# Loading the first tokens in two halves, casting in quarters, and a new order of issue in a fused attention and maxout kernel

## The chip, the cores and the metric

One core of one Trainium2 chip. The metric is the device time of one execution in microseconds (us), median of several runs. "Span" is the length of the profiled part of an execution; the device time of a run is 1.7 to 3.3 us longer than its span. A run has a state: "slow" runs (here those over 1.5% above the fastest of the same kernel) are kept out of every ratio. A ratio is the mean time of one kernel's fast runs over the mean of the other's fast runs of the same rounds, so it is not quite the ratio of the medians quoted beside it; the brackets are its 95% interval.

In the profiles PE is TensorE (the array that multiplies) and PEld its weight loads, DVE is VectorE, ACT is ScalarE, POOL is GpSimd, and SP is SyncE, which here only issues transfers. A transfer has "landed" when all of it has arrived. "Before" and "after" name the kernel before the change and the changed kernel.

## The reference

Cut to what matters:

```python
# x: (8, 8, 512, 64)   state: (8, 8, 32, 64)     B, H, S, Ns, D = 8, 8, 512, 32, 64
def _attn_ref(x, state):
    scores = scale * np.matmul(x, state.transpose(0, 1, 3, 2))
    a = softmax(scores)                      # over the 32 states
    xread = np.matmul(a, state)              # 512 rows a batch
    scores2 = scale * np.matmul(state, x.transpose(0, 1, 3, 2))
    a2 = softmax(scores2)                    # over the 512 tokens
    sread = np.matmul(a2, x)                 # 32 rows a batch
    return np.concatenate([xread, sread], axis=2)

def _moe_ref(x, w1, w2, w3, w_out):          # 4352 rows of 512, d_ff = 768
    h = np.maximum(np.maximum(x @ w1, x @ w2), x @ w3)
    return h @ w_out
```

## The kernel before

The kernel never forms `xread`. It multiplies the state into the three weight matrices once per batch (`M`), and a token's 32 softmax weights per head then meet that product directly (`u`). The work is cut into small units, and a text lists them in order. The first batches have a hand-found list (OPENING); later batches repeat PERIOD, and the end has LAST. No scheduler reorders anything: each engine runs its instructions in this order, so an instruction that waits holds up all behind it on its engine.

```python
OPENING = """
id, idle 9, sel, idle 9, pm 0 0 a, pm 0 1 v, lx 1, xT 0 0 v, lw 2 4, pm 1 1 v, pm 1 0 v,
xT 0 1 a, idle 8, lw 1 2, lw 0 1, S 0 0 g, S 0 1 g, xT 1 1 a, xT 1 0 a, R 0, lw 4 6,
S 1 1 g, aT 0 0 a, M 0 2 va, aT 0 1 v, S 1 0 g, M 0 3 aa, M 1 3 av, M 1 2 aa, M 2 1 vv,
u 0 3 0, u 0 3 1, M 0 1 aa, u 0 2 0, M 1 1 va, aT 1 - v, u 0 2 1, M 0 0 aa, R 1, u 0 1 0,
... (cut: seven more lines)
"""
```

The words:

- `idle n`: n matmuls on zeros (`pz`) that keep the array warm. `sel`: the state, transposed on PE into `pst` and copied into the block-diagonal `sbd`, two copies on ACT and two on DVE.
- `pm b h e`: cast or permute tokens of batch b into `xn` on engine e. `xT b h e`: transpose that half of `xn` on PE (`px`) and copy it out on e. `xb b`: the same for a whole batch by a DMA that transposes ("the crossbar"), issued from SP.
- `S b h g`: scores on PE (`ps`), exponential on ACT (`e`), sum and reciprocal on DVE (`den`, `rden`), product on GpSimd (`a`). `aT b`: `a` transposed on PE (`pa`). `ab b`: the same by the crossbar.
- `M b m`: state times column block m of the weights (`pm` on PE, copies to `M_sb` on two engines). `u b m i`: two matmuls (`pw`) and one step of the maximum. `o b j h`: half an output tile (`po`). `R b`: the reads of the states (`pr`).
- `lx b`, `lw m0 m1`, `lo`: loads of tokens, of weight columns and of the output weights, all issued by GpSimd and cast to bf16 on the way.

The two loads that do not come from GpSimd stand ahead of the list:

```python
    st32 = res.tile([128, Ns // 2, D], F32, name="st32")
    nc.sync.dma_start(
        out=st32.rearrange("p n d -> p (n d)"),
        in_=state.rearrange("b h (q n) d -> (b h q) (n d)", q=2))
    x32 = res.tile([128, H, J, D], F32, name="x32")
    nc.sync.dma_start(out=x32.rearrange("p h j d -> p h (j d)"),
                      in_=x[0].rearrange("h (p j) d -> p h (j d)", j=J))
    ...
    nc.scalar.copy(out=st16, in_=st32)

    def load_w(m0, m1):
        c = slice(m0 * 128, m1 * 128)
        for i in range(3):
            nc.gpsimd.dma_start(out=W[:, i, :, c], in_=w_v[i][:, :, c])

    def load_x(b):
        x_sb[b] = xlp.tile([128, H, J, D], BF16, tag="x", name="x")
        nc.gpsimd.dma_start(
            out=x_sb[b].rearrange("p h j d -> p h (j d)"),
            in_=x[b].rearrange("h (p j) d -> p h (j d)", j=J))
    ...
    def x_crossbar(b):
        nc.sync.dma_start_transpose(
            out=xT(b).rearrange("p j hp t -> p (j hp) t"),
            in_=x_nat(b).rearrange("p j h d -> p (j h) d"))
```

The softmax here doesn't subtract the row's maximum and nothing guards it: scores larger than these inputs give would overflow.

Of the kernel before, what the change touches and what calls it, by code (L numbers as in the profile page):

```python
# [8 lines left out]
F32 = mybir.dt.float32  # L9
# [15 lines left out]



OPENING = """
id, idle 9, sel, idle 9, pm 0 0 a, pm 0 1 v, lx 1, xT 0 0 v, lw 2 4, pm 1 1 v, pm 1 0 v,
xT 0 1 a, idle 8, lw 1 2, lw 0 1, S 0 0 g, S 0 1 g, xT 1 1 a, xT 1 0 a, R 0, lw 4 6,  # L30
S 1 1 g, aT 0 0 a, M 0 2 va, aT 0 1 v, S 1 0 g, M 0 3 aa, M 1 3 av, M 1 2 aa, M 2 1 vv,
u 0 3 0, u 0 3 1, M 0 1 aa, u 0 2 0, M 1 1 va, aT 1 - v, u 0 2 1, M 0 0 aa, R 1, u 0 1 0,
lx 3, u 1 1 0, u 0 2 2, u 0 0 0, u 1 1 1, M 0 5 aa, M 0 4 aa, lx 2, u 0 1 1, u 0 3 2, lo,
u 1 3 0, u 0 0 1, u 0 5 0, M 1 0 va, pm 2 - g, u 1 3 1, u 1 1 2, u 0 4 0, M 2 2 aa,
u 1 3 2, lx 4, u 0 5 1, pm 3 - g, u 1 0 0, M 2 5 aa, M 1 5 aa, xb 3, u 0 1 2, u 0 5 2,
u 1 2 0, xT 2 1 v, u 0 4 1, u 0 0 2, u 1 5 0, u 0 4 2, xT 2 0 a, u 1 0 1, S 2 1 g,
o 0 0 0 v, M 1 4 aa, M 2 3 aa, o 0 0 1 v, u 1 2 1, o 0 1 0 v, S 2 0 g, u 1 5 1, u 1 2 2,
o 0 1 1 a, o 0 2 0 v, o 0 2 1 a, M 2 0 aa, M 2 4 aa, aT 2 - v, u 1 4 0, u 1 0 2, u 1 5 2,
o 0 3 0 v, o 0 3 1 a, u 1 4 1, u 1 4 2, R 2
"""  # L40


PERIOD = """
u u u P L S S o o u M M m o u u o u u u o u u o X u M m m R u o u u u o u u
"""
LAST = """
u u u u u u M M u u u S u o u o u u M u u R u u M o u o S M L o M P o o X o
"""


# [1 line left out]
def kernel(  # L52
# [14 lines left out]
    nc = tc.nc  # L67

    B, H, S, D = x.shape
# [5 lines left out]
    J = S // 128  # L75
# [8 lines left out]
    res = ctx.enter_context(tc.tile_pool(name="res", bufs=1))  # L84
# [14 lines left out]
    def copy(eng, o, i):  # L99
        if eng == "a":  # L100
            nc.scalar.copy(out=o, in_=i)  # L101
        else:
            ENG[eng].tensor_copy(out=o, in_=i)  # L103
# [4 lines left out]
    def tr(out_ap, in_ap):  # L108
# [4 lines left out]



    st32 = res.tile([128, Ns // 2, D], F32, name="st32")
    nc.sync.dma_start(
        out=st32.rearrange("p n d -> p (n d)"),
        in_=state.rearrange("b h (q n) d -> (b h q) (n d)", q=2))

    x32 = res.tile([128, H, J, D], F32, name="x32")
    nc.sync.dma_start(out=x32.rearrange("p h j d -> p h (j d)"),
                      in_=x[0].rearrange("h (p j) d -> p h (j d)", j=J))
    zeros = const.tile([128, 512], BF16, name="zeros")
    nc.vector.memset(zeros, 0.0)  # L125
    sbd = res.tile([128, B, HP, 2, Ns], BF16, name="sbd")
# [2 lines left out]
    nc.vector.memset(ones, 1.0)  # L129
    ident = const.tile([128, 128], BF16, name="ident")  # L130
    st16 = res.tile([128, Ns // 2, D], BF16, name="st16")
    nc.scalar.copy(out=st16, in_=st32)


    W = res.tile([128, 3, HP, d_ff], BF16, name="W")
# [5 lines left out]
# [5 lines that stand above are left out]
    def load_wout():  # L146
        nc.gpsimd.dma_start(out=wout, in_=moe_w_out.rearrange("(kk p) f -> p kk f", p=128))

    x_sb = {}
# [8 lines that stand above are left out]
    def idle(n):  # L158
        pz = bank([128, S], F32, "pz")
        for _ in range(n):  # L160
            mm(pz, zeros[:, 0:128], zeros, True, True)


    def state_to_T():
        sel = ident.rearrange("p (q a k) -> p a q k", a=2, k=2)
        for half in range(2):
            pst = bank([128, 8, 64], F32, "pst")
            for n in range(8):
                for par in range(2):
                    mm(pst[par * 64:(par + 1) * 64, n, :], st16[:, 8 * half + n, :], sel[:, par],  # L170
                       n == 0, n == 7, pos=(0, par * 64))
            for par in range(2):
                r = slice(par * 64, par * 64 + 64)
                o = sbd[r, :, :, par, :].rearrange("p b hp (k n) -> p (b hp) k n", k=2)
                copy("av"[par], o[:, :, :, 8 * half:8 * half + 8],
                     pst[r].rearrange("p n (q k) -> p q k n", k=2))
# [17 lines left out]
    def tile_of(kind, b, pool, shape):  # L194
        if (kind, b) not in tiles:
            tiles[kind, b] = pool.tile(shape, BF16, tag=kind, name=kind)
        return tiles[kind, b]

    def x_nat(b):
        return tile_of("xn", b, xnp, [128, J, H, D])  # L200
# [12 lines left out]

    def permute_x(b, h, eng):
        j = slice(0, J) if h is None else slice(2 * h, 2 * h + 2)
        i = x_sb[b][:, :, j] if b else x32[:, :, j]
        copy(eng, x_nat(b)[:, j], i.rearrange("p h j d -> p j h d"))

    def x_crossbar(b):
        nc.sync.dma_start_transpose(  # L220
            out=xT(b).rearrange("p j hp t -> p (j hp) t"),
            in_=x_nat(b).rearrange("p j h d -> p (j h d)"))

    def x_array(b, h, eng):
        px = bank([128, 2, HP, 128], BF16, "px")
        for jj in range(2):
            for hp in range(HP):
                tr(px[:, jj, hp, :], x_nat(b)[:, 2 * h + jj, 2 * hp:2 * hp + 2, :])
        copy(eng, xT(b)[:, 2 * h:2 * h + 2], px)
# [118 lines left out]
    def issue(words):  # L348
        op_, args = words[0], words[1:]
        n = [None if v == "-" else int(v) for v in args if v == "-" or v.isdigit()]  # L350
        eng = args[-1] if args and args[-1].isalpha() else None
        if op_ == "idle":
            idle(*n)
        elif op_ == "id":
            make_identity(nc, ident)
        elif op_ == "sel":
            state_to_T()
        elif op_ == "lx":
            load_x(*n)
        elif op_ == "lw":  # L360
            load_w(*n)
        elif op_ == "lo":
            load_wout()
        elif op_ == "pm":
            permute_x(*n, eng)
        elif op_ == "xb":
            x_crossbar(*n)
        elif op_ == "xT":
            x_array(*n, eng)
        elif op_ == "S":  # L370
            scores(*n, eng)
        elif op_ == "R":
            state_reads(*n)
        elif op_ == "ab":
            a_crossbar(*n)
        elif op_ == "aT":
            a_array(*n, eng)
        elif op_ == "M":
            made.add(tuple(n))
            m_unit(*n, eng)  # L380
        elif op_ == "u":
            up(*n)
        else:
            out_half(*n, eng)

    for unit in OPENING.split(","):
        issue(unit.split())

    m_q = [(b, m) for b in range(2, B) for m in range(MT) if (b, m) not in made]
    for t in range(1, B):  # L390
        p, g = ORDER[t], ORDER[t + 1]
# [60 lines left out]
```

## Time and profile before

| before | |
|---|---|
| device time, median of 3 runs | 160.18 us (160.11 to 160.54) |
| span of the profiled run | 158.2 us |
| PE busy | 150.8 us |
| state, then x of batch 0, landed | 4.07, 7.66 us |
| first scores, second `a` done | 11.41, 15.65 us |
| first `pw` (the first unit `u`) | 18.04 us |
| start of the repeated part (its first `pw`, by the chain of waits) | 47.23 us |
| one period | 15.77 us |
| last matmul ends | 154.79 us |
| last matmul to the end of the span | 3.4 us |

Read it by milestones. Once PE has work without holes, everything later follows from how much work is left, so each cause can be placed between two milestones. The prediction below shows the lines behind the table.

### The profile page before, as it was taken

The numbers are of one execution on the slowest core, as the hardware profiler recorded it, in microseconds if no ns is written. First come the engines' busy times: TensorE is split into PE (matmuls) and PEld (weight loads), VectorE is DVE, ScalarE is ACT, GpSimd is POOL, SyncE is SP. The second block draws the span as 40 slices with busy tenths as digits, with TensorE's granted clock in tenths as the row PEclk, the third lists the DMA queues.
The fourth block names the chain that finished last, engine by engine and source line by source line (L and its number), as shares of the span: only waits on it lengthen the run. The fifth ranks groups of instructions, "written<-read, shape, count | busy, mean of one in ns | idle before, by whom it ended". The sixth has DMA issues, their size and how long they took to land.

```text
span 158.2 us, 3558 instructions
## 1 busy us (share of the span) xinstructions
PE 150.8 (95%) x1387; PEld 76.1 (48%) x1404; DVE 112.0 (71%) x200; ACT 94.8 (60%) x188; POOL 44.3 (28%) x48
## 2 busy tenths in 40 slices
PE   6988899999999999999999999999999999999991
PEld 2456353354454454445444544444445567754450
DVE  3358999797669788968886888688868834378601
ACT  3549978768546765676477647764777433344340
POOL 8927960282630920190018001300130000000000
PEclk9999999999999999999999999999999999999999
DMA  5999999979659498909991609260316033030253
GB/s 161 279 195 188 185 162 163 200 104 173 195 60 250 116 198 114 264 29 181 126 265 38 167 0 244 68 161 0 137 46 153 4 133 133 0 133 4 66 188 143
DMA packets 34400, 21.46 MB, mean 136 GB/s; under 512 B 19536, under 2 KB 31824, under 8 KB 34384
## 3 DMA queue, kind: packets, MB, share of 16 engines
q0 software_dynamic: 14400, 6.82, 34.0%
q1 hardware_dynamic: 19840, 14.29, 32.9%
q8 instruction: 11, 0.18, 0.4%
q10 hardware_dynamic: 144, 0.13, 0.2%
q14 instruction: 5, 0.04, 0.1%
HBM read 15.20 MB, written 8.91 MB: 152 GB/s over the span
## 4 chain that ended last, share of the span: by engine, by line
PE 88%; DMA 4%; ACT 2%; POOL 1%; issue 1%; DVE 1%; SPq 0%; POOLq 0%
PE pw L106 45%; PE po L106 28%; PE pm L106 6%; DMA x<-in_x_dram 4%; PE pr L106 4%; PE ps L106 2%; PE px L109 1%; POOL a L246 1%; PE pz L106 1%; PE pa L109 1%; ACT e L238 1%; ACT xn L101 1%; ACT M_sb L101 0%; DVE den L242 0%; DVE oh L103 0%
## 5 line engine op out<-in xcount | busy, mean ns | idle before, releaser
L106 PE MATMUL pw<-aT,M_sb 128*128 128x512 bf16 x288 | 71.9, 379 | 0.0
L106 PE MATMUL po<-wout,ht 128*128 128x512 bf16 (+1 forms) x194 | 51.1, 373 | 0.8
L304 DVE TENSOR_TENSOR t<-t,pw 128x512 bf16<-128x512 bf16 (+1 forms) x54 | 35.4, 656 | 19.6 <-PE pw L106 9.1
L300 ACT CAST t<-pw 128x512 bf16<-128x512 f32 (+1 forms) x54 | 30.5, 567 | 29.5 <-PE pw L106 28.6
L106 PEld LDWEIGHTS <-M_sb 128*128 128x128 bf16 x288 | 26.9, 98 | 31.5 <-issue 1.0
L306 DVE TENSOR_TENSOR ht<-t,pw 128x512 bf16<-128x512 bf16 (+1 forms) x54 | 35.2, 657 | 6.8 <-PE pw L106 3.0
L246 POOL TENSOR_TENSOR a<-e,rden 128x512 bf16<-128x512 bf16 x16 | 16.4, 1041 | 59.4 <-ACT e L238 36.6
L101 ACT CAST M_sb<-pm 128x384 bf16<-128x384 f32 x75 | 30.9, 504 | 1.3 <-PE pm L106 0.5
L106 PEld LDWEIGHTS <-ht 128*128 128x128 bf16 x210 | 19.6, 98 | 21.3 <-issue 1.9
L101 ACT COPY o<-po 128x512 f32<-128x512 f32 x32 | 18.8, 586 | 18.6 <-PE po L106 16.1
L103 POOL COPY xn<-x 128x2048 bf16<-128x2048 bf16 x6 | 11.3, 1887 | 8.1 <-DMA x<-in_x_dram 8.1
L106 PE MATMUL pm<-W,sbd 64*32 64x384 bf16 x384 | 12.4, 327 | 0.5 <-ACT M_sb L101 0.4
L242 DVE TENSOR_REDUCE den<-e 128x16 f32<-128x512 bf16 x16 | 10.6, 661 | 2.0 <-ACT e L238 1.9
L238 ACT ACTIVATE e<-ps 128x512 bf16<-128x512 f32 x16 | 8.9, 598 | 4.6 <-PE ps L106 4.6
L103 DVE CAST M_sb<-pm 128x384 bf16<-128x384 f32 x21 | 10.6, 534 | 0.0
L144 POOL DMA_DIRECT2D W<-in_moe_w_dram x12 | 9.0, 771 | 3.6 <-DMA x<-in_x_dram 3.0
L106 PE MATMUL pw<-AT,W 128*128 128x256 bf16 x72 | 9.2, 273 | 0.1
L106 PE MATMUL pz<-zeros 128*128 128x512 bf16 x25 | 7.8, 470 | 1.2 <-DVE zeros L125 1.2
L106 PEld LDWEIGHTS <-sbd 64*32 64x32 bf16 x384 | 4.3, 89 | 9.7 <-issue 9.1
L106 PEld LDWEIGHTS <-W 128*128 128x128 bf16 x72 | 7.0, 98 | 2.5
L279 DVE RECIPROCAL rd<-pr 128x128 f32<-128x128 f32 x8 | 7.6, 947 | 0.2 <-PE pr L106 0.2
L153 POOL DMA_DIRECT2D x<-in_x_dram x7 | 6.6, 942 | 0.1
(39 smaller groups left out, 67.6 us busy)
## 6 DMA issues: line engine op xcount, KB each, us to landing
out_dram<-o SPq DMA_DIRECT2D x14, 512.0 KB, 2.9
x<-in_x_dram POOLq DMA_DIRECT2D x7, 512.0 KB, 7.7
W<-in_moe_w_dram POOLq DMA_DIRECT2D x6, 256.0 KB, 8.0
x<-in_x_dram SPq DMA_DIRECT2D x1, 1024.0 KB, 6.5
W<-in_moe_w_dram POOLq DMA_DIRECT2D x6, 128.0 KB, 10.9
wout<-in_moe_w_out_dram POOLq DMA_DIRECT2D x1, 768.0 KB, 12.6
out_dram<-o SPq DMA_DIRECT2D x3, 256.0 KB, 2.1
st<-in_state_dram SPq DMA_DIRECT2D x1, 512.0 KB, 3.3
```

Source lines behind the costliest of these rows:

```text
L101: nc.scalar.copy(out=o, in_=i)
L103: ENG[eng].tensor_copy(out=o, in_=i)
L106: nc.tensor.matmul(out_ap, lhsT, rhs, start=start, stop=stop, tile_position=pos)
L144: nc.gpsimd.dma_start(out=W[:, i, :, c], in_=w_v[i][:, :, c])
L153: nc.gpsimd.dma_start(out=x_sb[b].rearrange("p h j d -> p h (j d)"), in_=x[b].rearrange("h (p j) d -> p h (j d)", j=J))
L238: nc.scalar.activation(out=e.rearrange("p r n -> p (r n)"), in_=ps.rearrange("p j a hp n -> p (j a hp n)"), func=AF.Exp, scale=scale)
L242: nc.vector.reduce_sum(out=den, in_=e, axis=AX.X)
L246: ENG[eng].tensor_mul(out=a_of(b)[:, 2 * h:2 * h + 2].rearrange("p j a hp n -> p (j a hp) n"), in0=e, in1=rden.unsqueeze(2).to_broadcast(( ...
L279: nc.vector.reciprocal(out=rd, in_=pd.rearrange("p (hp n) -> p hp n", hp=HP))
L300: nc.scalar.copy(out=t[:, :nn], in_=pw[:, :nn])
L304: nc.vector.tensor_max(t[:, :nn], t0[:, :nn], pw[:, :nn])
L306: nc.vector.tensor_max(ht[:, m, :nn], tiles["t", g, m][:, :nn], pw[:, :nn])
```

## The change

Its intent: get batch 0 through its softmax sooner, by letting casts and transposes of a first half of x begin while the rest still loads; take transposes of batch 2 off PE; and find the orders anew for that.

```diff
+    x32 = res.tile([128, H, J, D], F32, name="x32")
     st32 = res.tile([128, Ns // 2, D], F32, name="st32")
+    def load_x32(k):
+        nc.sync.dma_start(
+            out=x32[:, :, 2 * k:2 * k + 2, :].rearrange("p h j d -> p h (j d)"),
+            in_=x[0].rearrange("h (p k j) d -> k p h (j d)", k=2, j=2)[k])
+    load_x32(0)
     nc.sync.dma_start(
         out=st32.rearrange("p n d -> p (n d)"),
         in_=state.rearrange("b h (q n) d -> (b h q) (n d)", q=2))
-    nc.sync.dma_start(out=x32..., in_=x[0]...)          # (cut)
+    load_x32(1)
-    nc.scalar.copy(out=st16, in_=st32)
+    def permute_x32(h, q, eng):                          # "p0 h q e": a quarter of x
+        j, hh = slice(2 * h, 2 * h + 2), slice(4 * q, 4 * q + 4)
+        copy(eng, x_nat(0)[:, j, hh], x32[:, hh, j].rearrange("p h j d -> p j h d"))
+    def cast_state(h, eng):                              # "ca h e": half of the state
+        n = slice(8 * h, 8 * h + 8)
+        copy(eng, st16[:, n], st32[:, n])
 OPENING = """
-id, idle 9, sel, idle 9, pm 0 0 a, pm 0 1 v, lx 1, xT 0 0 v, lw 2 4, pm 1 1 v, pm 1 0 v,
-...
+id, idle 9, p0 0 0 v, p0 0 1 a, xT 0 0 v, lw 2 4, ca 0 a, idle 5, p0 1 0 a, ca 1 v, lx 1,
+p0 1 1 v, sel, lw 1 2, lw 4 6, xT 0 1 v, S 0 0 g, S 0 1 g, pm 1 1 g, lw 0 1, M 0 3 vv,
+M 1 2 aa, M 1 3 aa, pm 1 0 v, R 0, aT 0 0 a, M 0 2 aa, lx 2, xT 1 0 a, aT 0 1 v,
+xT 1 1 v, M 0 1 va, lx 3, u 0 2 0, u 0 2 1, S 1 1 g, S 1 0 g, u 0 3 0, u 0 1 0, u 0 1 1,
+M 0 5 av, lo, M 0 4 aa, M 1 1 aa, u 0 3 1, u 0 2 2, u 0 3 2, pm 2 - g, u 0 4 0, M 0 0 aa,
+... u 1 4 0, xb 2, u 0 5 1, M 2 1 aa,
+... o 0 0 0 a, u 1 2 1, S 2 0 g, S 2 1 g, o 0 0 1 a, o 0 1 0 v, o 0 1 1 a, u 1 0 1, ab 2,
+...                                                      (cut)
 PERIOD = """
-u u u P L S S o o u M M m o u u o u u u o u u o X u M m m R u o u u u o u u
+P u u u S o u u S L o o o u u u m M m o o u u m m M R X u u u u u o o u u u
```

LAST is reordered too.

More of the change, by code (lines that the diff above doesn't have):

```diff
@@ L28 @@
 OPENING = """
-id, idle 9, sel, idle 9, pm 0 0 a, pm 0 1 v, lx 1, xT 0 0 v, lw 2 4, pm 1 1 v, pm 1 0 v,
-xT 0 1 a, idle 8, lw 1 2, lw 0 1, S 0 0 g, S 0 1 g, xT 1 1 a, xT 1 0 a, R 0, lw 4 6,
-S 1 1 g, aT 0 0 a, M 0 2 va, aT 0 1 v, S 1 0 g, M 0 3 aa, M 1 3 av, M 1 2 aa, M 2 1 vv,
-u 0 3 0, u 0 3 1, M 0 1 aa, u 0 2 0, M 1 1 va, aT 1 - v, u 0 2 1, M 0 0 aa, R 1, u 0 1 0,
-lx 3, u 1 1 0, u 0 2 2, u 0 0 0, u 1 1 1, M 0 5 aa, M 0 4 aa, lx 2, u 0 1 1, u 0 3 2, lo,
-u 1 3 0, u 0 0 1, u 0 5 0, M 1 0 va, pm 2 - g, u 1 3 1, u 1 1 2, u 0 4 0, M 2 2 aa,
-u 1 3 2, lx 4, u 0 5 1, pm 3 - g, u 1 0 0, M 2 5 aa, M 1 5 aa, xb 3, u 0 1 2, u 0 5 2,
-u 1 2 0, xT 2 1 v, u 0 4 1, u 0 0 2, u 1 5 0, u 0 4 2, xT 2 0 a, u 1 0 1, S 2 1 g,
-o 0 0 0 v, M 1 4 aa, M 2 3 aa, o 0 0 1 v, u 1 2 1, o 0 1 0 v, S 2 0 g, u 1 5 1, u 1 2 2,
-o 0 1 1 a, o 0 2 0 v, o 0 2 1 a, M 2 0 aa, M 2 4 aa, aT 2 - v, u 1 4 0, u 1 0 2, u 1 5 2,
-o 0 3 0 v, o 0 3 1 a, u 1 4 1, u 1 4 2, R 2
+id, idle 9, p0 0 0 v, p0 0 1 a, xT 0 0 v, lw 2 4, ca 0 a, idle 5, p0 1 0 a, ca 1 v, lx 1,
[3 more added lines that the diff above has]
+M 0 5 av, lo, M 0 4 aa, M 1 1 aa, u 0 3 1, u 0 2 2, u 0 3 2, pm 2 - g, u 0 4 0, M 0 0 aa,
+u 0 1 2, aT 1 - v, u 0 4 1, M 1 4 aa, M 1 0 av, u 0 4 2, u 0 0 0, u 1 1 0, u 0 5 0,
+u 1 1 1, u 0 0 1, u 1 3 0, u 1 0 0, u 0 0 2, u 1 3 1, u 1 4 0, xb 2, u 0 5 1, M 2 1 aa,
+M 2 4 aa, pm 3 - g, M 1 5 vv, u 0 5 2, u 1 1 2, u 1 2 0, u 1 3 2, xb 3, u 1 5 0,
+o 0 0 0 a, u 1 2 1, S 2 0 g, S 2 1 g, o 0 0 1 a, o 0 1 0 v, o 0 1 1 a, u 1 0 1, ab 2,
+M 2 2 aa, M 2 5 aa, u 1 0 2, R 1, o 0 2 0 v, o 0 2 1 a, u 1 4 1, lx 4, u 1 5 1, M 2 0 va,
+M 2 3 aa, R 2, u 1 4 2, u 1 2 2, o 0 3 0 v, u 1 5 2, o 0 3 1 a
 """
 PERIOD = """
-u u u P L S S o o u M M m o u u o u u u o u u o X u M m m R u o u u u o u u
+P u u u S o u u S L o o o u u u m M m o o u u m m M R X u u u u u o o u u u
 """
 LAST = """
-u u u u u u M M u u u S u o u o u u M u u R u u M o u o S M L o M P o o X o
+u u M u M M u X M M u P u u u u o u u u L u o u u u S S R u o u o M o o o o
 """
@@ L119 @@
         in_=state.rearrange("b h (q n) d -> (b h q) (n d)", q=2))
-    x32 = res.tile([128, H, J, D], F32, name="x32")
-    nc.sync.dma_start(out=x32.rearrange("p h j d -> p h (j d)"),
-                      in_=x[0].rearrange("h (p j) d -> p h (j d)", j=J))
+    load_x32(1)
     zeros = const.tile([128, 512], BF16, name="zeros")
@@ L215, in permute_x @@
         j = slice(0, J) if h is None else slice(2 * h, 2 * h + 2)
-        i = x_sb[b][:, :, j] if b else x32[:, :, j]
-        copy(eng, x_nat(b)[:, j], i.rearrange("p h j d -> p j h d"))
+        copy(eng, x_nat(b)[:, j], x_sb[b][:, :, j].rearrange("p h j d -> p j h d"))
+    def permute_x32(h, q, eng):
[4 more added lines that the diff above has]
+        copy(eng, st16[:, n], st32[:, n])
     def x_crossbar(b):
@@ L363, in issue @@
             load_wout()
+        elif op_ == "ca":
+            cast_state(*n, eng)
+        elif op_ == "p0":
+            permute_x32(*n, eng)
         elif op_ == "pm":
```

## The prediction

> **What bounds the kernel now.** I read the page first, then the chain of waits, the DMA of single microseconds, and the timeline of the opening. The page's busy row and its slices:
>
> ```profile
> PE 150.8 (95%) x1387; PEld 76.1 (48%) x1404; DVE 112.0 (71%) x200; ACT 94.8 (60%) x188; POOL 44.3 (28%) x48
> ...
> PE   6988899999999999999999999999999999999991
> ...
> DMA  5999999979659498909991609260316033030253
> ```
>
> PE has work in every slice from the sixth to the last but one; the first five, some 20 us, are not full although part of their work is filler (`pz` on zeros). The chain of waits says where PE takes over:
>
> ```profile
> 1.20 6.46 DMA x<-in_x_dram
> 7.68 1.05 ACT xn L101
> 8.78 1.07 PE px L109 x16
> ...
> 14.61 1.05 POOL a L246
> 15.71 0.40 PE pa L109 x4
> 16.10 0.25 PE ps L106 x8
> 16.37 0.60 ACT e L238
> 16.97 0.76 ACT M_sb L101 x2
> 17.75 0.36 PE pm L106 x8
> 18.11 0.97 PE pw L106 x4
> ```
>
> Until 18.11 the chain hops between DMA, casts, softmax and transposes; from there to 154.8 it is PE, back to back. So the time is (end of the last hole in PE) + (work then left on PE) + (a tail of 3.4 us of copy and store). The change can only gain by closing holes before 18 us or by taking work off PE.
>
> A second limit hides there. The landings of the weights (start of issue plus time to landing, asked one issue at a time):
>
> ```profile
> x<-in_x_dram POOLq DMA_DIRECT2D x1, 512.0 KB, 9.0
> ...
> W<-in_moe_w_dram POOLq DMA_DIRECT2D x1, 256.0 KB, 10.5
> ...
> W<-in_moe_w_dram POOLq DMA_DIRECT2D x1, 128.0 KB, 11.4
> ...
> W<-in_moe_w_dram POOLq DMA_DIRECT2D x1, 256.0 KB, 6.7
> ```
>
> x of batch 1: 1.43 + 9.0 = 10.4. Third piece of W for column blocks 2 and 3 (call it W23): 3.98 + 10.5 = 14.5. Third piece of block 1 (W1): 6.21 + 11.4 = 17.7. W0, by the same sum, 19.9. W45: 17.1 + 6.7 = 23.8. M_sb of block 1 first runs at 17.75, just when W1 lands. The queue that GpSimd feeds is full from 7 to 22 us:
>
> ```profile
> q1 hardware_dynamic: 92, 0.09, 103.9%
> q0 software_dynamic: 3, 0.00, 4.5%
> ...
> q0 software_dynamic: 788, 0.39, 145.4%
> ```
>
> The first two rows are 6.25 to 6.5 us, the third 10 to 12. The GpSimd queue moves nothing until the SP queue's 1.5 MB of state and x runs out, then 0.195 MB/us as counted on the bf16 side.
>
> **What the Trainium skill says.** "DMA: Bandwidth & Descriptors", section "Issuing engines are not separate DMA queues": all issuers share the 16 engines and interleave. The trace agrees on the sharing, but shows the SP queue served nearly alone first. The same page, "Why small descriptors are slow (HBM only)", gives a fixed 3 cycles per packet; halving x's runs from 1024 to 512 bytes would then cost (16+3)/16 against (32+3)/32, 9%. Here W1's small pieces ran at 714 packets per us in 16 to 17 us, 512 bytes read each, 365 GB/s, so I expect little loss. "VectorE: DVE Perf Modes", "The three transpose paths": a DMA transpose avoids PE but is slower in itself (1309 against 390 ns per 128x128). Here the crossbar of xT takes 4.4 to 6.7 us to land, all beside PE. "TensorE: Matmul & The Clock Gate", "What's actually happening": the array starts at half clock until busy some 3.4 us. Here the first 9 fillers took 4.02 us, the next 8 1.90; 9 fillers are kept at the start, so the array should be warm as before.
>
> **The change part by part.**
>
> 1. Head. The order of SP's queue becomes half of x, state, half of x. State and x landed at 4.05 and 7.66; the three equal pieces should land near 4.2, 6.0 and 7.8. Casts in quarters: 1024 columns took 1.04 us on ACT, 0.69 on DVE; half as many I estimate at 0.62 and 0.43 (slopes from 512- and 1024-column copies of aT). First half of x: cast by 4.9, transposed once the 9 fillers end at 5.2, copied by 6.5 on DVE. State: cast 6.0 to 7.0, 5 fillers, transposes 6.9 to 7.9. Second half of x: cast 7.8 to 8.5. But the two sbd copies on each engine stand behind these casts: DVE 8.3 to 9.6. Scores then start at 9.65 (before: 11.41), the second half after its xT copy at 10.35. The whole softmax chain moves up by about 1.8 us: second `a` done at 13.8 instead of 15.65.
>
> 2. GpSimd's queue. W23 goes ahead of x1, and W45 ahead of W0; bytes up to W1 are the same. At the old pace: W23 11.8 (was 14.5), x1 14.5 (was 10.4), W1 17.7 (as before), W45 17.7 + 0.786/0.195 = 21.7 (was 23.8), W0 about 24 (was 19.9).
>
> 3. PE in its new order, which cannot overtake. M 0 3, M 1 2, M 1 3 (8 matmuls, 0.25 to 0.29 us each) start at 11.8; R 0 takes 0.92, the first aT and M 0 2 end at 14.3. The array then waits for x1, cast and transposed by 16.2, then in M 0 1 for W1: 17.75. The first `pw` is at about 18.05, as now. Five `u` (0.43 each) and two scores (0.47) fill to 20.7; M 0 5 waits for W45 until 21.7, a hole of 1.0 us that the old order lacks.
>
> 4. Work taken from PE: 16 transposes of x and 8 of `a` for batch 2 go to the crossbar. They stand in the chain as 0.58, 0.45 and 0.55 us: 1.58 us gone. 12 of 26 fillers go too, but lay in holes.
>
> Sum: from M 0 5 at 21.7 to the end of the opening remain 31 `u` at 0.4315 (13.4), 13 M (3.2), 8 half outputs at 0.65 (5.2), two R (1.75), two scores (0.47), one aT (0.55): 24.6, so 46.3, plus 0.4 for changes of shape as the old opening shows (22.6 measured against 22.05 added up): 46.7. The old opening ends at 47.23. Gain 0.5 us.
>
> 5. The repeated period. It holds 18 `u`, 8 half outputs, 6 M, R and two scores in both orders: 7.77 + 5.18 + 1.22 + 0.92 + 0.47 = 15.56 by the chain's pieces, against 15.77 from 67.21 to 82.98. At most 0.2 us a period is there to win. DVE gets one more M copy (0.53) per period, 12.7 to 13.2 of 15.77; walking the new order I find its backlog behind R at 2 us, three or four of eight banks, hence no stall. Tail: the last `u`, halves and stores are the same. I put 0 on both.
>
> **The rivals.** (a) The earlier softmax is worth its full 1.8 us, plus the 1.58: 156.8. For it: the chain shows softmax ahead of 18.11. Against: W1 lands at 17.7 whatever the softmax does. It needs the loads to be quicker than I think. (b) Weights bind harder: W0 is now last, or small runs slow the head; M 0 0 waits beyond 24, and each microsecond of lateness is one of time: 161 to 162. (c) The crossbar for batch 2 is late: x2 lands near 26.5, GpSimd copies it (1.89), and with 6.3 to 6.7 to landing it ends near 35; scores of batch 2 stand at 35.5. Only about 0.5 us of slack; wout (34.3 before) meets `po` at 34.4 just as tightly. A slip would cost up to 1 us. (d) The new period runs worse, DVE at 84%: 0.2 us each in five periods, plus 1.0.
>
> **Range and chances.** My sum gives 160.2 - 0.5 = 159.7; (b) to (d) push up by perhaps 0.3, while an order found anew presumably survived some measure of its finder, and (a) in part would give 1 us or more. I choose 159.4. The landings of W1 and W45 carry plus or minus 0.8 each, which gives 157.8 to 160.8 for 8 in 10. Faster by over 2% needs below 157.0, all of (a) with no new hole: 0.08. Slower by over 2%, above 163.4, needs (b) and (c) together: 0.02. Within 2%: 0.90.
>
> **What would show it.** Right: first scores near 9.7; W23 landed near 11.8, W45 near 21.7; the first `pw` within 0.5 us of 18.1; holes in PE before M 0 1 and M 0 5 ending with W; the period at 15.7 to 15.8; 24 fewer transposes on PE. Wrong: `pw` starting below 17 with no hole at M 0 5 (rival a), a hole at `ps` of batch 2 or at the first `po` (c), or a period that differs by over 0.1 (d, or an unlooked-for gain). My prediction falls if the weights land over 1 us from my sums, since all of it hangs on their cumulative bytes.

## The result

| | before | after |
|---|---|---|
| device time, median of 6 runs each, same rounds | 160.5 us (160.11 to 160.8) | 162.18 us (161.97 to 163.44) |
| ratio | | 1.0117 [1.0084, 1.0151] |
| second half of x landed (before: all of x) | 7.66 | 9.83 |
| first scores, second `a` done | 11.41, 15.65 | 12.34, 16.77 |
| first `pw` | 18.04 | 19.05 |
| start of the repeated part | 47.23 | 48.31 |
| one period | 15.77 | 15.77 |
| last matmul ends | 154.79 | 155.92 |
| last matmul to the end of the span | 3.4 | 4.2 |
| device time less span, mean | 1.77 | 2.52 |

The changed kernel is slower, within 2%. The loss is 1.9 us (0.0117 of 160.4). In means over runs it has two parts: the span grows by 1.16 us (158.68 in the 28 runs of the kernel before that stand beside the experiments, 159.84 in 7 of after), and 0.75 us more lies between span and device time. (The 0.75 is uneven: two of the seven runs have 3.2 and 3.3 us outside the span, the other five 2.1 to 2.4.) In the one profiled pair the last matmul ends 1.13 us later, of which 1.08 is already there at 48.31, and then the stretch from the last matmul to the end of the span is 0.8 us longer as well. These add up to more than the mean loss, so one trace does not settle how the 1.16 divides between the opening and that stretch.

The page of after, its busy row and its slices (40 equal slices, busy share in tenths; PEclk is the granted clock of the array):

```profile
PE 148.1 (92%) x1353; PEld 74.6 (47%) x1368; DVE 115.3 (72%) x207; ACT 90.8 (57%) x180; POOL 45.9 (29%) x49
...
PE   7718999998999999999999999999999999999990
...
PEclk9985799999999999999999999999999999999999
```

PE has 2.7 us less to do than before and ends later. The third slice (8 to 12 us) is nearly empty, where the kernel before had an 8, and the granted clock is 0.5 from 10.8 to 17.7 us (the digits are means of slices).

The chain that ended last in after, the stretches to 21 us and from 21 to 49 us (start, length, what it waited on or did):

```profile
1.88 7.96 DMA x<-in_x_dram
...
10.99 1.31 DVE sbd L105 x2
...
12.34 0.60 PE ps L108 x8
...
15.73 1.04 POOL a L260
16.77 1.18 POOL xn L105
17.95 2.25 POOL W L151 x3
20.19 0.85 POOL x L160
21.04 8.81 DMA x<-in_x_dram
29.85 6.98 DMA xT<-xn
36.83 0.05 issue
36.88 0.64 PE ps L108 x16
...
46.98 1.30 DVE ht L320 x2
...
48.31 0.81 PE pw L108 x3
```

Before, the chain left the start at 18.11 and stayed on PE. Now it leaves PE again. The late second half of x (1.88 + 7.96 = 9.84) delays the columns of the state, the scores and `a`. GpSimd makes `a`, and behind `a` stand GpSimd's permute of batch 1 and its issue of the next loads. So the load of batch 2 is issued at 20.2 and lands at 27.9; the 8.81 of the chain includes GpSimd's permute of it, 1.89 us, to 29.85. Then comes the crossbar, 6.98 us to landing, and PE waits for it. One late transfer at the start costs a second time at 37 us, by way of a queue on GpSimd.

What PE waited for in after, up to 50 us (total, times, longest):

```profile
PE px L111 <- ACT xn L103: 2.8, 1, 2.8
...
PE ps L108 <- DVE sbd L105: 1.0, 1, 1.0
PE ps L108 <- DMA xT<-xn: 0.7, 1, 0.7
...
PE po L108 <- DMA wout<-in_moe_w_out_dram: 0.3, 1, 0.3
PE pw L108 <- DVE ht L320: 0.3, 1, 0.3
```

The first is the wait for the second half. The last three lie after the first `pw` and sum to 1.27 us unrounded (0.67, 0.31, 0.29). The last ends at 48.31, just after DVE's step (48.28) and the landing of the crossbar of `a` (41.27 + 6.9 = 48.17); the profile names the later one. No line names the weights: PE comes too late to wait for them. They landed at 11.9 (blocks 2 and 3), 16.8 (block 1), 21.3 (4 and 5) and 23.6 (0).

### The profile page after: what moved, and what is told of

Its sections match the earlier page's. It is cut to its first block, busy times and chain, and to the rows that moved or that the text cites. A ratio compares the mean times of both kernels' runs of the same rounds, so it can differ in the third digit from the quotient of the medians.

```text
span 160.1 us, 3487 instructions
## 1 busy us (share of the span) xinstructions
PE 148.1 (92%) x1353; PEld 74.6 (47%) x1368; DVE 115.3 (72%) x207; ACT 90.8 (57%) x180; POOL 45.9 (29%) x49
## 4 chain that ended last, share of the span: by engine, by line
PE 72%; DMA 15%; POOL 4%; DVE 3%; issue 1%; ACT 1%; SPq 1%; POOLq 0%
PE pw L108 36%; PE po L108 26%; DMA x<-in_x_dram 10%; PE pm L108 4%; DMA xT<-xn 4%; PE pr L108 4%; PE ps L108 2%; POOL W L151 1%; POOL a L260 1%; DVE sbd L105 1%; DVE ht L320 1%; POOL xn L105 1%; DVE rd L293 1%; POOL x L160 1%; DVE den L256 0%
## 5 line engine op out<-in xcount | busy, mean ns | idle before, releaser
L108 PE MATMUL pw<-aT,M_sb 128*128 128x512 bf16 x288 | 69.3, 379 | 0.4 <-DVE ht L320 0.3
L108 PE MATMUL po<-wout,ht 128*128 128x512 bf16 (+1 forms) x195 | 48.7, 373 | 1.1 <-DMA wout<-in_moe_w_out_dram 0.3
L318 DVE TENSOR_TENSOR t<-t,pw 128x512 bf16<-128x512 bf16 (+1 forms) x54 | 34.9, 649 | 10.3 <-ACT t L314 6.0
L103 ACT COPY o<-po 128x512 f32<-128x512 f32 x33 | 19.3, 586 | 25.0 <-PE po L108 24.0
L103 ACT CAST M_sb<-pm 128x384 bf16<-128x384 f32 x68 | 27.9, 499 | 2.6 <-PE pm L108 2.6
L105 POOL COPY xn<-x 128x2048 bf16<-128x2048 bf16 (+1 forms) x7 | 12.6, 1793 | 32.3 <-DMA x<-in_x_dram 16.8
L105 DVE CAST M_sb<-pm 128x384 bf16<-128x384 f32 x28 | 14.4, 549 | 0.5
L108 PE MATMUL pw<-AT,W 128*128 128x256 bf16 x72 | 8.7, 273 | 0.0
L108 PEld LDWEIGHTS <-xT 128*128 128x128 bf16 x128 | 5.8, 102 | 5.2 <-issue 1.2
L108 PE MATMUL ps<-sbd,xT 128*128 128x64 bf16 x128 | 6.4, 199 | 1.8 <-DVE sbd L105 1.0
## 6 DMA issues: line engine op xcount, KB each, us to landing
wout<-in_moe_w_out_dram POOLq DMA_DIRECT2D x1, 768.0 KB, 10.8
```

What stands on the lines that cost most here:

```text
L103: nc.scalar.copy(out=o, in_=i)
L105: ENG[eng].tensor_copy(out=o, in_=i)
L108: nc.tensor.matmul(out_ap, lhsT, rhs, start=start, stop=stop, tile_position=pos)
L318: nc.vector.tensor_max(t[:, :nn], t0[:, :nn], pw[:, :nn])
```

## The experiments

Fifteen kernels ran, all with correct results. Unless said otherwise an edit is made to the changed kernel.

| run | what it is | median, us | ratio to before | first `pw` | last matmul ends |
|---|---|---|---|---|---|
| e1 | before's PERIOD and LAST | 161.26 | 1.0055 [0.9985, 1.0125] | | 156.13 |
| e2 | 12 more fillers | 162.83 | 1.0142 [1.0052, 1.0232] | 19.04 | |
| e3 | state's columns before the casts | 160.79 | 1.0043 [0.9980, 1.0105] | 18.44 | 154.47 |
| e4 | split loads and casts only | 162.66 | 1.0141 [1.0071, 1.0211] | 20.08 | 157.53 |
| e5 | more stores in the period | 162.54 | 1.0105 [1.0051, 1.0159] | | |
| e6 | new orders only | 160.54 | 0.9989 [0.9929, 1.0049] | 16.91 | 153.85 |
| e7 | halves cut by heads (one run, state unknown) | 166.33 | none | | |
| e8 | a new order, first try | 163.93 | 1.0206 [1.0154, 1.0257] | 16.38 | |
| e9 | weights issued after x's second half | 160.93 | 1.0051 [0.9996, 1.0106] | 17.95 | 153.91 |
| e10 | batch 2's transposes back on PE | 161.37 | 1.0082 [1.0033, 1.0132] | | 155.62 |
| e11 | a new order, second try | 163.03 | 1.0153 [1.0083, 1.0223] | 16.65 | 157.08 |
| e12 | e6 with blocks 4 and 5 later | 160.55 | 1.0025 [0.9979, 1.0071] | | 154.75 |
| e13 | e9 and e10 together | 160.8 | 1.0004 [0.9961, 1.0046] | 18.2 | 155.2 |
| e14 | a new order, third try | 162.7 | 1.0030 [0.9962, 1.0098] | (slow profile) | |
| e15 | only the crossbar of `a` back on PE | 162.16 | 1.0109 [1.0047, 1.0172] | 18.5 | 154.3 |

Milestones come from one profiled execution each, so they vary as runs do. I use them to compare mechanisms, and the ratios to compare kernels. Between two of these kernels a difference of ratios under some 0.6% is within the intervals.

### Which half of the change: e4 and e6

e4 takes the split loads and the quarter casts, with the lists of before:

```diff
 OPENING (of before, with only its head changed)
-id, idle 9, sel, idle 9, pm 0 0 a, pm 0 1 v, lx 1, xT 0 0 v, ...
+id, idle 9, ca 0 a, ca 1 v, sel, idle 9, p0 0 0 v, p0 0 1 a, p0 1 0 a, p0 1 1 v, lx 1, xT 0 0 v, ...
```

> The kernel before with only the loads in halves and the casts in quarters, all its orders kept. Theory A: x's second half lands near 9.8 instead of 7.7 because GpSimd's loads share with it, state at 6.0 instead of 4.05; first scores 11.9 instead of 11.4, time 160.9 to 161.3. Rival (the new order alone is at fault, the head is harmless or helps): 159.5 to 160.5.

e6 is the reverse: before's two loads, its whole cast of the state and its head, then the new lists from there on:

```diff
-id, idle 9, p0 0 0 v, p0 0 1 a, xT 0 0 v, lw 2 4, ca 0 a, idle 5, p0 1 0 a, ca 1 v, lx 1,
-p0 1 1 v, sel, lw 1 2, lw 4 6, xT 0 1 v, S 0 0 g, ...
+id, idle 9, sel, idle 9, pm 0 0 a, pm 0 1 v, lw 2 4, xT 0 0 v, lx 1, lw 1 2, lw 4 6, xT 0 1 a, S 0 0 g, ...
```

> The other half of the two by two: loads, casts and state's columns of the kernel before (state, then x whole, fillers as before), all orders from the second batch on, repeated and last period as in the changed kernel. Theory A (the loads in halves and the casts ahead of the columns are what costs): x at 7.7, first scores near 11.4, weights' block 1 at 17 to 17.7, first pw near 18, holes at M 0 1 and M 0 5 that end with weights, last matmul 0.3 to 0.8 us earlier than the kernel before's, time 159.4 to 160.4 (the tail 0.6 to 0.8 longer). Rival (the new order is at fault): 161.2 or more.

The split alone is the harmful half. In e4 x's second half landed near 10.2, the last matmul came 2.7 us later than in the kernel before, and the time rose by 1.4%. (Here the state comes second and `sel` is first on PE, so its PE was late as well, and the next eight fillers took 3.31 us, where they took 1.90 in before. So e4 is not the late half of x alone.) The orders alone end PE 0.94 us earlier than before, which the time does not show (0.9989, an interval of plus or minus 0.6%): from the last matmul to the end of the span its trace has 4.2 us instead of 3.4, which takes most of the 0.94 away again. So the new orders were not bad; in the changed kernel they met a head that was late. In e6 the first `pw` is at 16.91 and there is the weight hole that the prediction had placed at M 0 5. What PE waited for in e6, up to 50 us:

```profile
PE pm L105 <- DMA W<-in_moe_w_dram: 1.5, 2, 1.3
```

### Why the second half landed at 9.8: e7 and e9

Two theories. By the size of the pieces (512-byte runs instead of 1024 are slow), or by the order of issue: in after GpSimd starts to issue weights before SP issues the second half. The timeline of the first microseconds of after (start, length, issuing engine):

```profile
0.74 0.46 SPq L123 DMA_DIRECT2D x<-in_x_dram  x1
...
1.27 0.56 SPq L128 DMA_DIRECT2D st<-in_state_dram  x1
...
1.43 2.43 POOL L151 DMA_DIRECT2D W<-in_moe_w_dram  x3
...
1.88 0.43 SPq L123 DMA_DIRECT2D x<-in_x_dram  x1
```

e7 cuts x by heads instead of tokens, so that its runs stay at 1024 bytes; it is slow by design elsewhere, since each half now needs both casts:

```diff
-            out=x32[:, :, 2 * k:2 * k + 2, :].rearrange("p h j d -> p h (j d)"),
-            in_=x[0].rearrange("h (p k j) d -> k p h (j d)", k=2, j=2)[k])
+            out=x32[:, 4 * k:4 * k + 4].rearrange("p h j d -> p h (j d)"),
+            in_=x[0, 4 * k:4 * k + 4].rearrange("h (p j) d -> p h (j d)", j=J))
```

> The changed kernel with x of batch 0 split by heads instead of by token columns: runs of 1024 bytes as in the kernel before, otherwise the same bytes and issues (the casts then fit the halves worse, its time is of no interest). Theory D (the shared engines take turns by packets, so runs of half the size give the SP queue half the share once GpSimd's loads are there): the second half lands at 7.9 to 8.5 us instead of 9.8. Rival (turns by bytes, or the later start alone): 9.3 to 10.

It landed at 9.4 with the larger pieces too (one execution): the size of the pieces is not the cause of the 2 us. e9 holds GpSimd back instead, with a fill of an unused tile ahead of its first load:

```diff
-... xT 0 0 v, lw 2 4, ...
+... xT 0 0 v, gm, lw 2 4, ...
+        elif op_ == "gm":
+            junk = const.tile([128, 1280], BF16, name="junk")
+            nc.gpsimd.memset(junk, 0.0)
```

> The changed kernel with one GpSimd memset of about a microsecond ahead of its first load, so that all three loads of SP are issued (the third at 1.88 us) before the first load of GpSimd. Theory F (the engines take the two queues in the order of issue: the second half of x comes late because the weights were issued at 1.43, ahead of it): second half of x lands at 7.9 to 8.5 instead of 9.8, scores near 10.8 instead of 12.3, time 161.0 to 161.6. Rival (the share is by packets whatever the order of issue): 9.5 to 10, scores 12.3, time 162 or more.

The timeline of e9, same stretch:

```profile
1.25 1.16 POOL L378 MEMSET junk<- 128x1280 bf16 x1
...
1.88 0.43 SPq L123 DMA_DIRECT2D x<-in_x_dram  x1
...
2.36 1.68 POOL L151 DMA_DIRECT2D W<-in_moe_w_dram  x2
```

Now the queues in the one microsecond from 6 to 7 (packets, MB, share of the 16 engines; q1 is what SP issued, q0 what GpSimd issued), first after, then e9:

```profile
q1 hardware_dynamic: 297, 0.15, 63.4%
q0 software_dynamic: 172, 0.09, 63.4%
```

```profile
q1 hardware_dynamic: 562, 0.28, 93.7%
q0 software_dynamic: 76, 0.04, 28.4%
```

In after x and the weights share this microsecond evenly; in e9, x has most of it, and from 7 to 8 it has 13 packets left (in after 187, and 179 more from 8 to 9). x landed at 8.2 in e9. The other two kernels with the same fill landed it at 9.0 (e13) and about 7.4 (e14); the ones with halves and without it at 9.4 to 10.2. So holding GpSimd back is worth some 1.6 us on average (8.2 against 9.8), with 0.8 us of variation from run to run. Is it the order, or only that GpSimd starts 0.93 us later (2.36 instead of 1.43)? e9 changes both. From 6 to 6.5 us GpSimd's queue moved 80 packets in after and 2 in e9. It moved only 3 to 18 in the five kernels with whole loads (before, e6, e8, e11, e12), where GpSimd is not held back but SP's last issue, at 1.20, is ahead of it; there all of x landed at 7.66 to 8.39. That speaks for the order, though no run moves the order alone. The weights paid little for it: blocks 4 and 5 landed at 20.86 against 21.3, but block 1 at 17.5 against 16.8, and PE now waited 1.1 us for weights. The first `pw` came at 17.95 instead of 19.05 and the last matmul 2.0 us earlier. The ratio fell by 0.7%, which is just outside the noise, and the kernel is level with the kernel before, not ahead, although its opening ended at 46.29 and its last matmul 0.9 us earlier than before's (153.91 against 154.79). From the last matmul to the end of the span it has 4.2 us instead of 3.4, and outside the span 2.35 instead of 1.77. And the halves land at best (7.4, in e14) about where the whole x landed (7.66).

### Where the columns of the state stand: e3 and e2

In after the casts of x's second half stand ahead of `sel` on both engines, so the state's columns wait for a load that they do not need.

```diff
-... idle 5, p0 1 0 a, ca 1 v, lx 1, p0 1 1 v, sel, ...
+... idle 5, ca 1 v, lx 1, sel, p0 1 0 a, p0 1 1 v, ...
```

> The changed kernel with the state's cast, transposes and its four column copies issued ahead of the casts of x's second half. Theory A: columns done by 9.5 instead of 12.3, first scores near 11.3 (now behind x's second transposes, since x still lands at 9.8), first pw near 18.0 instead of 19.05; time 161.2 to 161.6. Rival (what counts is only the landing of x's second half): no change, 162.1.

Scores came at 10.82 and 11.77, the first `pw` at 18.44, and now the weights bind. What PE waited for in e3, up to 50 us:

```profile
PE pm L108 <- DMA W<-in_moe_w_dram: 1.8, 2, 1.2
```

1.5 us of earlier softmax gave 0.6 us at the first `pw`, and 1.8 us went into two waits for weights. That is the second limit of which the prediction spoke; the head had hidden it. (Block 1 also landed later in this execution, at 18.0 against 16.8.)

The gain did not stop there. The second `a` was done at 15.06 instead of 16.77, so GpSimd issued the load of batch 2 earlier (20.16 in after):

```profile
18.45 1.79 POOL L160 DMA_DIRECT2D x<-in_x_dram  x2
```

It landed at 26.6 instead of 27.9, PE no longer waited for the crossbar of x, and the opening ended at 46.85 instead of 48.31. The last matmul came 1.45 us earlier than in after, and the ratio, 1.0043, is as good as that of e9, although x's second half still landed at 9.67. So the late half of x cost what it did because the state's columns stood behind its casts; moving either one gives more than half of the loss back.

PE idles 2.8 us in after (7.7 to 10.5), and its granted clock is 0.5 from 10.8 to 17.7 us. Does the cold array cost? e2 puts 12 fillers into the hole:

```diff
-p0 1 1 v, sel, lw 1 2, ...
+p0 1 1 v, sel, idle 12, lw 1 2, ...
```

> The changed kernel with 12 more fillers between the state's transposes and the second transposes of x, so that PE has no empty stretch from 7.7 to 10.5 us. Theory A: granted clock 1.0 throughout, first scores still near 12.3 (they wait for the state's columns), but scores 0.25 instead of 0.60 us and later work at full pace; time 0.4 to 0.8 us less than the changed kernel, 161.3 to 161.8. Rival (the cold array is the whole loss): 160.3 to 160.7. Rival (cold array is hidden behind softmax): 162.1.

The clock stayed at 1.0, scores came at 12.53 and the first `pw` at 19.04 against 19.05. So PE reached the first `pw` no earlier with a warm array in that stretch. The ratio, 1.0142, gives no gain; its profile fell in a slow run, and only the milestones of the opening are used.

### The work taken off PE: e10, e13 and e15

```diff
-... u 1 4 0, xb 2, u 0 5 1, ...
+... u 1 4 0, xT 2 0 v, xT 2 1 a, u 0 5 1, ...
-... u 1 0 1, ab 2,
+... u 1 0 1,
-M 2 3 aa, R 2, ...
+M 2 3 aa, aT 2 - v, R 2, ...
```

> The changed kernel with batch 2's x and a transposed on PE as in the kernel before (24 transposes and four copies put back, two crossbar transfers gone). If PE's work is what ends the opening: the waits for xT (0.67) and for aT at the first pw of batch 2 (0.3) go, 1.58 of work comes, the repeated period starts near 48.9 instead of 48.3, time 162.4 to 162.9. Rival (the chain x2, copy, crossbar, scores, a, crossbar ends the opening, and PE has room): period near 47.3 to 47.8, time 161.0 to 161.7.

With 1.58 us of transposes back on PE, the opening ended at 48.16 instead of 48.31, and no wait is left in it after the first `pw`. What PE waited for in e10, up to 50 us:

```profile
PE px L111 <- ACT xn L103: 2.7, 1, 2.7
PE pz L108 <- DVE zeros L133: 1.2, 1, 1.2
PE ps L108 <- DVE sbd L105: 1.2, 1, 1.2
PE px L111 <- DVE xn L105: 0.3, 1, 0.3
```

So in the changed kernel the crossbars bought nothing: 1.58 us of work was replaced by 1.27 us of waits, and what the rest should have been worth did not arrive either. The ratio fell by 0.35%, which is within the noise.

e13 joins e9 and e10:

> Two edits that were each tried alone before: the weights issued after the second half of x (that run measured 1.0051 and its last matmul ended at 153.91 us), and batch 2's transposes back on PE (1.0082, 155.62). Theory 'the part of the time outside the span needs split loads and the two crossbars together': the time less the span is near 1.9 us here, as in the runs that lack either. Theory 'the crossbar chain ended the opening': with the head repaired the chain had only 0.4 us of wait left in the opening, so giving PE 1.58 us back should cost about 0.8 us: last matmul ends near 154.6. Rival: with an earlier head the transposes are hidden still, and it ends at 153.9. Ratio to the kernel before near 1.003, at 154.6.

It is level with the kernel before: 1.0004. It recovers 1.13% of the changed kernel, clear of the noise; the sum of the two repairs, 0.66% (e9) and 0.35% (e10), is of that size, but the second is too small to be seen alone. Against my expectation its last matmul ended at 155.2, not 154.6: in profiles with a good head the crossbars do end PE earlier (153.9 in e9), but the device time did not follow, since e9 has 2.35 us between span and device time and e13 1.93.

e15 gives back only the transpose of `a`:

> The changed kernel with only the transpose of a of batch 2 back on PE; that of x stays on the crossbar. Asks which of the two crossbars goes with the time outside the span: if the one of a, the time less the span is near 1.9 us (ratio near 1.008); if the one of x, it stays near 2.5 (ratio near 1.012). On PE: four transposes' 0.55 us come back, and the wait of 0.3 us before the first pw of batch 2 goes; period start between 48.0 and 48.5 by either theory.

The opening ended 1.5 us earlier than in after, against my expectation of 48.0 to 48.5:

```profile
46.82 1.29 PE pw L108 x6
```

No wait for a crossbar is left in this trace. Part of that is the execution and not the edit: x's second half landed at 9.44 here and the load of batch 2 at 26.3, where after has 9.83 and 27.9. PE's gain was not to be seen in the time: this trace has 5.0 us from the last matmul to the end of the span. The time less the span fell from 2.52 to 1.77, the value of the kernel before, but the mean span rose from 159.84 to 160.35 and the time did not move (1.0109). So that extra goes with the crossbar of `a` in this pair, yet taking it away is worth nothing by itself.

### The period, the tail and the time outside the span: e1 and e5

e1 puts PERIOD and LAST of before under the new opening:

```diff
-P u u u S o u u S L o o o u u u m M m o o u u m m M R X u u u u u o o u u u
+u u u P L S S o o u M M m o u u o u u u o u u o X u M m m R u o u u u o u u
```

> The changed kernel with the repeated and the last period of the kernel before. Theory A (the loss comes from the opening: second half of x lands late, state's columns wait behind its casts, the array cools): periods took 15.77 us in both traces, so the time stays at 162.0 to 162.5. Rival P (the new last period costs the 0.8 us by which the span's end moved more than the last matmul did, 1.9 against 1.1): 161.2 to 161.5, last store landing 2.9 us after its issue instead of 3.7.

The last matmul ended at 156.13 against 155.92: the new period and ending did not make PE late, and the stretch behind the last matmul stayed at 4.2 us. The ratio, 1.0055, has an interval that includes both no difference and the changed kernel's 1.0117; it tells little.

In the trace of after 4.2 us lie between the last matmul and the end of the span, against 3.4 before. I guessed that this came from which semaphore the last store happens to use, and shifted it with five more stores:

```diff
-            if j % 2 == 1:
+            if j % 2 == 1 and j == 1 and 1 <= g <= 5:
+                for jj in range(2):
+                    nc.sync.dma_start(out=rows[jj], in_=o[:, jj, :])
+            elif j % 2 == 1:
```

> The changed kernel with five output stores in the middle issued as two halves each, so that the last stores signal on the same semaphores as in the kernel before (the change has three more transfers on SP, which moved them on by three). Theory T (the last 0.8 us of the loss is the end of the program: it waits for the transfers' semaphores one by one, and is longer when the last store holds one of the first of them): from the end of the last output copy's issue to the end of the span 3.4 us as before instead of 4.2, time 161.2 to 161.6. Rival (chance, or the new last period): still 4.2, time 162.

The tail in the trace did fall to 3.4 us, and the device time did not: 2.56 us lay between it and the span on average. The guess fits this one trace and is worthless for the time.

Mean time less span over all runs: 1.77 to 1.93 in before, e4, e6, e8, e10 to e15; 2.12 to 2.56 in after, e1, e2, e3, e5 and e9, and 2.23 in the single run of e7. The second group is exactly the kernels with split loads and both crossbars of batch 2. What happens there is outside the trace and stays open.

Inside the span, the stretch from the last matmul to the end is 3.4 us in before and e5, 3.8 in e4, e10, e13 and e14, 4.1 to 4.2 in after, e1, e3, e6, e7, e9 and e12, and 4.4 to 5.0 in e2, e8, e11 and e15 (the profiles of e2 and e14 are slow ones). So every variant but e5 loses 0.4 to 1.5 us there against before, and a kernel whose PE ends up to 0.9 us earlier is no faster for it. What sets this stretch was not found.

### Attempts at a better version: e8, e11, e12, e14

All four are new orders. e8 has the whole loads of before with the casts in quarters, e11 and e12 the loads and the casts of before, e14 the fill of e9 with the order of e3, batch 2's transposes on PE and later waits for weights. Their lists differ in too many places to be shown; e12's edit is the smallest, on top of e6:

```diff
-u 0 1 1, M 0 5 av, lo, M 0 4 aa, M 1 1 aa, u 0 3 1, u 0 2 2, u 0 3 2, pm 2 - g, ...
+u 0 1 1, M 1 1 aa, u 0 3 1, u 0 2 2, u 0 3 2, M 0 5 av, lo, M 0 4 aa, pm 2 - g, ...
```

> A version built from the findings: state, then x whole, casts in quarters on two engines, weights of blocks 2 and 3 ahead of x1, then blocks 1, 4 and 5, x2, block 0; every pw that needs only loaded weights ahead of those that wait; batch 2's x by crossbar, its aT on PE. Expected if weights and in-order waits are the limit: scores at 9.8 and 10.5, first pw near 14.6 to 15.5, the repeated period starts near 43 to 45 instead of 47.2 (before) and 48.3 (changed), time 156.5 to 158.5. If VectorE binds the long runs of pw: 158.5 to 160.

> A version from the findings: head and loads of the kernel before, weights of blocks 2 and 3 first, x2 issued ahead of block 0, every pw ahead of the M that waits for later weights, batch 2's x by crossbar and its aT on PE, copies spread over VectorE and ScalarE. Expected: first pw near 15.6 to 16.5, no wait for weights or crossbars over 0.3 us, repeated period from 43.5 to 45.5 (before 47.2, order-only 46.2), time 157.2 to 159.0. If copies on ScalarE or VectorE bind as in the first attempt: 159.5 to 161.

> The order-only kernel with M 0 5 and M 0 4 moved behind one M and three pw that have their weights already. Theory A (in-order PE waits for weight blocks 4 and 5: 1.34 us in order-only): that hole goes, yet the first pw of batch 2 still waits for the crossbar of aT, which follows the crossbar of xT landing at 34.4 just as the scores want it: so the last matmul moves by only 0 to 0.4 us, time 159.9 to 160.5. Rival (the hole is all that counts): 1.3 us earlier, 159.0 to 159.3.

> Attempt at the best of all: weights issued after x's second half, state's columns before the casts of that half, u of block 3 ahead of the wait for W1, the wait for W45 put later, batch 2's transposes on PE. Theory 'after the head only the weights bind': scores near 10.3, first pw near 17.3, holes on W of at most 0.5 us, last matmul ends near 153.7, time near 159.8 and ratio 0.996. Rival 'an earlier head meets the copies of M on ScalarE or the weights instead, as in the two attempts before': waits for M_sb on ACT or for W of 1 us or more, last matmul at 154.8 or later, ratio 1.003 or more.

None beats the kernel before. e8 started `pw` at 16.38, 1.7 us earlier than before, and gave it all back: ScalarE, which had the copies of `M`, of `xT` and of `aT`, made PE wait 1.8 us for `aT` and 1.0 for `xT`, and the repeated part began at 49.7. e11 moved copies to DVE and waited there instead (1.4 us for `M_sb`, 1.1 for `xn`). e12 closed the hole for blocks 4 and 5, and met waits of 0.8 us for `M_sb` and 0.7 for an output copy on ACT; its x also landed at 8.38, 0.7 later than in before for the same two loads. e14's profile and two of its four runs are slow; its two fast ones (160.92 and 161.49) tell only that it is no clear gain. In these four openings PE waited in turn for ScalarE, DVE and the weights: each gain met another limit.

## Why the prediction was wrong, point by point

The direction was wrong by little, the size by more: a gain of 0.5 us was added up, a loss of 1.7 in the medians came. By its own steps:

- **Part 1, the head: the step that failed.** "The three equal pieces should land near 4.2, 6.0 and 7.8." They landed at 4.73, 5.95 and 9.83. The prediction had seen the queue of SP served alone first, and took this for a property of the queue ("moves nothing until the SP queue's 1.5 MB of state and x runs out"). The quarter of a microsecond that it shows, with 3 packets of GpSimd's, is right, but from 6.5 to 7 GpSimd already had 76 of 180, with x still landing. In the kernel before both loads of SP were issued before GpSimd's first at 1.43; the change pushes a third issue to 1.88, behind it, and the two queues shared the engines while most of that half still had to move. e9 turned this order round and x landed at 8.2. The costs of the casts were right (0.62 and 0.43 us, as estimated), and so was the note that the copies of `sbd` stand behind them. Scores came 2.7 us later than predicted, the second `a` 3.0, and the first `pw` at 19.05 instead of 18.05. e3 shows that the note deserved more than a note: with the columns moved ahead of these casts more than half of the loss is gone.
- **Part 2, the weights: right.** Predicted 11.8, 17.7, 21.7 and 24; measured 11.9, 16.8, 21.3 and 23.6. One reading behind it was loose: the matmul that stands at 17.75 in before waited, by the profile, for a copy of ScalarE (0.4 us), and not for W1, whose last piece was issued at 6.17 (not 6.21) and landed at 17.6. In these runs PE waits for weights only where the head is earlier.
- **Part 3, PE's order: right where it arrived in time.** M 0 5 was put at 21.7 and ran at 21.77, but the hole of 1.0 us ahead of it was not there: PE reached it that late by itself. That the number fits is luck. Nor was there a hole ahead of M 0 1. Holes that end with weights appear in e6 (1.3 us the longest) and e3 (1.2 us), where the head is early.
- **Part 4, work taken from PE: the other step that failed.** The sum from M 0 5 to the end of the opening was 25.0; it took 48.31 - 21.77 = 26.5. Of these 1.5 us, 1.27 are the three waits. Rival (c) had named two of them and gave "only about 0.5 us of slack", from x of batch 2 landing "near 26.5". It landed at 27.9, since its issue stood behind the late `a` on GpSimd, and the crossbar then took 6.98. The rival was the right one, and it entered the estimate only as a share of "perhaps 0.3". The sum itself was sound: where the load of batch 2 came in time, the same stretch took 46.85 - 21.81 = 25.0 (e3) and 46.29 - 20.91 = 25.4 (e9).
- **Part 5: right for the period** (15.77 in both). The tail was put at 0. From the start of the repeated part to the last matmul the two kernels differ by 0.05 us, but in the traces 0.8 us more lies between the last matmul and the end of the span, and on average 0.75 more outside the span. The prediction counted the first as fixed (its "tail of 3.4 us") and did not speak of the second; both causes are open. This matters for the sign: with the head mended, e9 and e3 end their openings at 46.3 and 46.9, near the predicted 46.7, and are still not faster than the kernel before.
- **The cold array** came about against the statement that "the array should be warm as before": 2.8 us of idling were followed by a granted clock of 0.5, which the fillers of e2 prevented. It cost nothing that e2 could find.
- **The argument that a searched order "presumably survived some measure of its finder"** pulled the estimate to 159.4, below its own sum of 159.7. Against it, the new orders are level with the old ones when tried alone (e6).

Adding the terms: predicted opening 46.7, measured 48.31, 1.6 us; later work 0.05; outside the span 0.75. That is 2.4 of the 2.5 us between the sum (159.7) and the median (162.18). The fit is better than it should be: the trace's 0.8 us between the last matmul and the end of the span is left out, and the kernel before alone differed by 0.3 us between the two sets of runs.

What is shown: the second half lands late because GpSimd's loads are issued ahead of it, not because of its small pieces (e7 and e9, with the queues; order and delay not separated by one edit); the head with its split loads is the harmful part (e4 against e6); and the crossbars of batch 2 return nothing in the changed kernel (e10); head and crossbars both mended bring it level (e13). The way from the late `a` through GpSimd's queue to the late load of batch 2 is in the chain of after, and e3 and e9 bear it out: with `a` earlier, that load landed at 26.6 and 25.7, and PE did not wait for the crossbar of x. What stays open: the stretch behind the last matmul, inside and outside the span, which took up what e3, e6 and e9 gained on PE over the kernel before.

## What to carry to other kernels

Cutting a load into pieces adds issues, and here the issue that slipped 0.45 us behind another engine's first load landed 2 us late: compare the start times of all issues on the timeline before counting on a piece's landing. When work is moved from the busiest engine to a transfer, follow that transfer back to what issues it; if the issue stands in a queue behind the very work that is late, the saving turns into a wait. And when an opening is close to several limits at once, a milestone gained early is no gain until the next limits, and the time behind the last matmul, have been checked with numbers.

## What the Trainium skill lacked or had wrong

- "DMA: Bandwidth & Descriptors", section "Issuing engines are not separate DMA queues", says that transfers started by different engines interleave on the same 16 engines. The runs agree. What the skill lacks is how the order of issue bears on the shares, which were far from equal: in after, with GpSimd's weights issued 0.45 us ahead, x had 297 of 469 packets from 6 to 7 us and landed at 9.83; issued 0.48 us ahead of the weights, it had 562 of 638 and landed at 8.2 (the fill that did this also delayed the weights by 0.93 us).
- "Perfetto Trace Analysis", section "DMA Optimizations", says that splitting a DMA may let some of it start sooner, and the whole complete sooner if the engines are generally idle. Here they were full (the two queues' shares from 6 to 7 us sum to 127%), and the split's last piece landed 2.2 us later than the whole had (9.83 against 7.66); with the order of issue mended, between 7.4 and 9.0.
- No page tells why the device time outside the span of a trace should differ between two kernels that move the same inputs and outputs. Here it was 1.77 us on average for the kernel before and 2.52 for the changed one, with no cause that these runs could find. The same holds for the stretch from the last matmul to the end of the span, 3.4 to 5.0 us.
